# One load over 128 partitions, an earlier first product, and paired half-width products in a three-stage kernel

## The chip, the cores and the metric

The kernel runs on one core of a Trainium2 chip. The metric is the device time in microseconds of one execution. The time before is the median of three runs. A profile of one execution, taken by the hardware profiler, goes with it.

The engines are called TensorE (PE in the profile; PEld is its weight load), VectorE (DVE), ScalarE (ACT), GpSimd (POOL) and SyncE (SP). SyncE issues most of the transfers here.

## The reference

The reference has three stages. The first is a gated linear attention with a state per batch and head; the second sends each token to one of eight experts; the third is a dense gated block.

```python
B, H, S, D = 4, 8, 768, 48
f = 1.0 / (1.0 + np.exp(-f_logit))
for t in range(S):
    state = f[:, :, t, :, None] * state + np.einsum('bhd,bhe->bhde', k[:, :, t], v[:, :, t])
    y[:, :, t] = np.einsum('bhd,bhde->bhe', q[:, :, t], state)
x = y.transpose(0, 2, 1, 3).reshape(3072, 384)
...
logits = normalized(x) @ normalized(expert_emb).T / tau          # 8 experts
expert_idx = argmax(logits); gate_w = softmax(logits)[expert_idx]
out[tokens of e] = gate_w * (relu(x @ w1[e]) @ w2[e])            # 384 -> 1024 -> 384
...
return (out @ w_a) * (out @ w_b) @ w_out                         # 384 -> 1536 -> 384
```

All inputs and the output are float32.

## The kernel before

**Stage 1, attention (until about 137 us).** The 768 positions of 4 batches are cut into 24 blocks of 128 positions, numbered g = 0 to 23: chunk g // 4 of batch g % 4. A block holds 8 heads in 4 pairs; the two heads of a pair lie in partitions 0 to 47 and 64 to 111. The order of the work on each engine is written out by hand, and each engine works through its own list in that order.

For block g: `load_a` (L188) brings q, k and f, two transfers of 48 partitions each, into a ring of four tiles whose remaining partitions are filled once by memsets (`clear`, L552). `load_b` (L196) brings v. `tanh` (L202) and `gate_f` (L206) make the gate from f; the second of them runs on ScalarE for the first three blocks and on GpSimd after. `scan_b` (L218) is a backward scan on VectorE and, on GpSimd, the scaled k (kt). `scan_r` (L229) is a forward scan, `q_scale` (L237) the scaled q (qc), both on VectorE. `scores` (L269) makes two banks of scores on TensorE, one per head of a pair. `mask_a` (L279) copies one bank on ScalarE and masks it on GpSimd; `mask_v` (L292) masks the other on VectorE. `turn_k` (L253) transposes kt, `evac_k` (L262) copies the transpose out. `inter` (L300) is the product with the state, `intra` (L307) that of the masked scores with v, both into one bank, which `evac_y` (L314) copies out. `u_part` (L319) makes the addition to the state; `s_scale` (L244) and `s_add` (L328) update the state. `turn_y` (L337) turns the block's output so that tokens lie in partitions, and makes the eight logits with it. `x_copy` (L367) copies the rows out, `x_sq` (L361) makes each row's sum of squares on ScalarE, `x_lg` (L372) the logits.

The loop starts at L629. Iteration g does the scans of block g + 2, the scores and masks of g + 1, the products of g and the turn of g - 1. A few blocks at a time form a round: `route` (L385), a list of small VectorE steps with a few rank products on TensorE, which `tick` (L542) advances a step at a time, finds each token's place; `scatter_row` (L456) then sends 128 rows to `slots` in memory by an indirect transfer on GpSimd's queue. Before that, `zero_fill` (L623) has written zeros to parts of `slots`. Between them, weights of the first expert are loaded (`w_load`, L116) and split in two parts (`w_hi` on ScalarE, `w_lo` on VectorE).

The kernel starts with memsets, first loads, and 18 products on constants (`warm_up`, L347). Then come the scans of blocks 0 and 1 and the scores of block 0, before the loop is entered.

**Early experts (about 137 to 158 us).** The first 224 rows of expert 0 are worked on while the last rows are still on their way: `early_h` (L499), `early_split` (L507), `early_y` (L512), in turn for j = 0 to 7, between them the last round, the counts of all experts (L747 to L749) and the order of the experts.

**Stage 2, experts (L1103, 64 steps), and stage 3 (L1229).** A step of stage 2 has a product with w1 (`h_part`), its relu on ScalarE and a remainder on VectorE (`h_split`, L1006), and the product of the step before with w2 (`y_part`, L1020). Rows of the next expert are loaded from `slots` and turned meanwhile (`rows_load`, `x_turn`, `ids_copy`).

Of the kernel before, what the change touches and what calls it, by code (L numbers as in the profile page):

```python
# [18 lines left out]
L = 128  # L19
# [29 lines left out]
def build(tc, I, out, dbg=None):  # L49
# [23 lines left out]
    ids0 = epool.tile([HP, 2, XO], F32, name="ids0")  # L73
    half = epool.tile([128, NT // 128], F32, name="half")
    a0 = epool.tile([128, KC, XT], F32R, name="a0")
    XE = [a0[:, :, i * EN:(i + 1) * EN] for i in range(2)]
    pcs = epool.tile([1, 2, 128], F32, name="pcs")
# [65 lines left out]
    with tc.manual_schedule():  # L143
# [44 lines left out]
        def load_a(g, eng=(SP, SP), parts=False):  # L188
            if g < NG:
                qkf = qkf_t[g % NQ]  # L190
                for c in ((slice(2, 3), slice(0, 2)) if parts else (slice(0, 3),)):
                    for i in range(2):
                        eng[i].dma_start(out=qkf[64 * i:64 * i + D, c], in_=I["qkf"][g, i, :, c])
                st[g] = dict(qkf=qkf)

        def load_b(g, eng=SP):  # L196
            if g < NG:
                vx = in_p.tile([128, H, D], F32, tag="vx", name="vx", bufs=4)
                eng.dma_start(out=vx, in_=I["vx"][g])
                st[g].update(vx=vx)  # L200

        def tanh(g):  # L202
            if g < NG:
                A.activation(out=Fb[g % 2][:, :, 0:L], in_=st[g]["qkf"][:, 2], func=ACTF.Tanh, scale=0.5)

        def gate_f(g):  # L206
            if g < NG:
                F = Fb[g % 2]
                if g < 3:
# [8 lines left out]
        def scan_b(g):  # L218
            if g >= NG:
# [3 lines left out]
            V.tensor_tensor_scan(out=fl(Bt)[:, ::-1], data0=Fx[g % 2][:, 1:n1 + 1][:, ::-1], data1=fl(pat)[:, ::-1],  # L223
                                 initial=0.0, op0=ALU.mult, op1=ALU.add)
# [67 lines left out]
        def mask_v(g):  # L292
# [3 lines left out]
            pm = at_p.tile([128, NP, L], F32, tag="pm0", name="pm0")  # L296
            V.tensor_tensor(out=pm, in0=d["ps"][0], in1=mask.unsqueeze(1).to_broadcast([128, NP, L]), op=ALU.mult)
            d["pm0"] = pm
# [38 lines left out]
        def turn_y(g):  # L337
# [6 lines left out]
            for p in range(NP):  # L344
                T.matmul(out=xt[:, p], lhsT=d["yS"][:, p], rhs=pick[0:HP, p], start=True, stop=True)
# [21 lines left out]
        def x_copy(g, rd):  # L367
            i, xt = rd["n"], st[g]["x"]
# [69 lines left out]

        def rows_load(e):
# [48 lines left out]
        def early_turn():  # L488
            V.tensor_copy(ids0, rows[0:HP, 0:2, 0:XO])
# [51 lines left out]

        def tick(n=1):  # L542
# [9 lines left out]
        def clear(i, *eng):  # L552
            for c, e in zip((2, 1, 0), eng):
                e.memset(qkf_t[i][:, c], 30.0 if c == 2 else 0.0)

        V.memset(qkf_t[0][:, 2], 30.0)
        G.memset(qkf_t[0][:, 0:2], 0.0)
        load_a(0, (SP, A), True)
# [17 lines left out]
        clear(2, G, G, G)  # L576
        load_a(2)
        load_b(1)
# [6 lines left out]
        clear(3, G, G, G)  # L585
# [7 lines left out]
        q_scale(0)  # L593
        tanh(1)
# [847 lines left out]
```

## Time and profile before

| | |
|---|---|
| median of 3 runs | 831.11 us (829.69 to 831.29) |
| the profiled execution | 832.62 us, its span 830.9 us |
| mean granted TensorE clock | 0.994 of full |
| TensorE busy | 810.6 us (98%) |
| VectorE, ScalarE, GpSimd busy | 397.7, 331.1, 222.3 us |
| moved by DMA | 76.74 MB, mean 92 GB/s |

A row of the timeline gives the start, the duration, the engine, the line, the tiles (out<-in) and shapes, and in square brackets how long the engine was idle before it and what ended that. Instructions of one kind that follow each other are merged (x16). A row of windows gives the busy time of each engine in a stretch, in the order PE, PEld, DVE, ACT, POOL, then the granted clock as a share of full speed, the mean busy share of the 16 DMA engines, and GB/s.

### The profile page before, as it was taken

How to read it: one execution, taken by the hardware profiler on the slowest of the kernel's cores; microseconds unless marked ns; L12 is line 12 of the kernel's file. 1: busy time of each engine (PE TensorE's matmuls, PEld its weight loads, DVE VectorE, ACT ScalarE, POOL GpSimd, SP SyncE). 2: the span in 40 equal slices, each digit the busy share in tenths (PEclk: the TensorE clock that was granted, in tenths of full speed). 3: DMA queues.
4: the chain of work that ended last, by engine and by line, in shares of the span. 5: the costliest groups of instructions: out<-in, count | busy, mean ns of one | idle time of the engine just before them, and what ended most of it. 6: DMA issues, size and time to landing. Idle time of an engine off the chain costs nothing. (4 is left out here: it accounts for less than half of the span.)

```text
span 830.9 us, 13077 instructions
## 1 busy us (share of the span) xinstructions
PE 810.6 (98%) x5156; PEld 727.7 (88%) x5156; DVE 397.7 (48%) x696; ACT 331.1 (40%) x636; POOL 222.3 (27%) x237
## 2 busy tenths in 40 slices
PE   6999999999999999999999999999999999999996
PEld 4888888999999999998888888888888888888886
DVE  7999996545555454487873213212322321222222
ACT  4787885354544554444442122222221222222211
POOL 6648674235454644440001000100010010001001
PEclk8999999999999999999999999999999999999999
DMA  9999962554465545433411000100010010001001
GB/s 177 233 283 244 217 188 78 181 163 146 153 180 189 163 134 179 156 91 109 136 53 39 0 1 1 39 0 1 1 39 1 0 39 1 1 0 39 1 1 41
DMA packets 38490, 76.74 MB, mean 92 GB/s; under 512 B 7481, under 2 KB 20391, under 8 KB 38423
## 3 DMA queue, kind: packets, MB, share of 16 engines
q1 hardware_dynamic: 35223, 65.99, 28.5%
q0 software_dynamic: 3072, 9.56, 3.3%
q8 instruction: 42, 0.69, 0.3%
q10 hardware_dynamic: 128, 0.30, 0.1%
q14 instruction: 25, 0.20, 0.1%
HBM read 63.58 MB, written 12.25 MB: 91 GB/s over the span
## 5 line engine op out<-in xcount | busy, mean ns | idle before, releaser
L988 PE MATMUL pa<-a,w 128*128 128x512 f32 (+1 forms) x438 | 171.8, 392 | 0.0
L987 PE MATMUL pa<-a,w 128*128 128x512 f32 (+1 forms) x438 | 171.6, 392 | 0.0
L989 PE MATMUL pa<-a,w 128*128 128x512 f32 (+1 forms) x438 | 171.5, 392 | 0.0
L1175 DVE TENSOR_TENSOR rows<-rows,pa 128x512 f32<-128x512 f32 (+1 forms) x73 | 49.6, 679 | 241.3 <-PE pa L989 234.9
L1205 POOL DMA_INDIRECT out<-yT,idx x24 | 23.5, 979 | 430.4 <-ACT yT L1203 424.0
L1169 ACT ACTIVATE rows<-pa 128x512 f32<-128x512 f32 (+1 forms) x73 | 43.3, 593 | 168.8 <-PE pa L989 168.7
L1176 ACT ACTIVATE gh<-rows 128x512 fp32r<-128x512 f32 x71 | 44.9, 633 | 149.4 <-DVE rows L1175 149.4
L989 PEld LDWEIGHTS pa<-a,w 128*128 128x128 f32 x438 | 82.3, 188 | 19.3
L987 PEld LDWEIGHTS pa<-a,w 128*128 128x128 f32 x438 | 82.3, 188 | 16.1
L988 PEld LDWEIGHTS pa<-a,w 128*128 128x128 f32 x438 | 82.1, 187 | 16.2
L1192 PE MATMUL pq<-w,gl 128*128 128x384 f32 x284 | 95.3, 336 | 0.0
L1191 PE MATMUL pq<-w,gh 128*128 128x384 f32 x284 | 95.3, 336 | 0.0
L1190 PE MATMUL pq<-w,gh 128*128 128x384 f32 x284 | 95.3, 336 | 0.0
L867 POOL TENSOR_TENSOR w<-raw,w 128x512 fp32r<-128x512 f32 x48 | 73.0, 1543 | 40.6 <-ACT w L864 36.0
L1030 PE MATMUL po<-hh,w 128*128 128x224 f32 (+7 forms) x384 | 80.3, 344 | 0.0
L1179 DVE TENSOR_TENSOR gl<-rows,gh 128x512 fp32r<-128x512 f32 x71 | 49.1, 691 | 44.1 <-ACT gh L1176 42.7
L1030 PEld LDWEIGHTS po<-hh,w 128*128 128x128 f32 x384 | 66.6, 189 | 1.5 <-ACT hh L1010 0.3
L987 PE MATMUL ph<-a,w 128*128 128x224 f32 (+7 forms) x192 | 65.5, 341 | 0.1
L989 PE MATMUL ph<-a,w 128*128 128x224 f32 (+7 forms) x192 | 65.3, 340 | 0.0
L988 PE MATMUL ph<-a,w 128*128 128x224 f32 (+7 forms) x192 | 65.3, 340 | 0.0
L1010 ACT ACTIVATE hh<-ph 128x224 fp32r<-128x224 f32 (+7 forms) x64 | 31.5, 492 | 81.2 <-PE ph L989 78.2
L1011 DVE SCALAR_TENSOR_TENSOR hl<-ph,hh 128x224 fp32r<-128x224 f32 (+7 forms) x64 | 35.7, 558 | 45.4 <-ACT hh L1010 44.8
(245 smaller groups left out, 1326.8 us busy)
## 6 DMA issues: line engine op xcount, KB each, us to landing
raw<-moe_w SPq DMA_DIRECT2D x32, 768.0 KB
qkf<-qkf SPq DMA_DIRECT2D x44, 288.0 KB
vx<-vx SPq DMA_DIRECT2D x24, 192.0 KB
raw<-moe_w_a SPq DMA_DIRECT2D x6, 768.0 KB
raw<-moe_w_b SPq DMA_DIRECT2D x6, 768.0 KB
raw<-moe_w_out SPq DMA_DIRECT2D x6, 768.0 KB
slots<-raw SPq DMA_DIRECT2D x8, 295.5 KB
rows<-slots SPq DMA_DIRECT2D x2, 344.8 KB
```

Of the source, the lines that this page charges most:

```text
L867: (G if i < NPOOL else V).tensor_tensor(out=wt[:, 1, f], in0=raw[:, f], in1=wt[:, 0, f].bitcast(F32), op=ALU.subtract)
L987: T.matmul(out=out, lhsT=wh, rhs=xh, start=first, stop=False)
L988: T.matmul(out=out, lhsT=wl, rhs=xh, start=False, stop=False)
L989: T.matmul(out=out, lhsT=wh, rhs=xl, start=False, stop=last)
L1030: T.matmul(out=OS[e][k], lhsT=w[:, j % 4, k * 128:(k + 1) * 128], rhs=x, start=(j == 0 and w is wh and x is hh), stop=(j == FJ - 1 and x i ...
L1169: A.activation(out=ab[:, r], in_=pa, func=ACTF.Copy)
L1175: V.tensor_tensor(out=ab[:, r], in0=ab[:, r], in1=pp[1], op=ALU.mult)
L1176: A.activation(out=gh[:, r], in_=ab[:, r], func=ACTF.Copy)
L1179: V.tensor_tensor(out=gl[:, r], in0=ab[:, r], in1=gh[:, r].bitcast(F32), op=ALU.subtract)
L1190: T.matmul(out=q, lhsT=gh[:, c], rhs=wh[:, f % 4], start=(f == 0), stop=False)
L1191: T.matmul(out=q, lhsT=gh[:, c], rhs=wl[:, f % 4], start=False, stop=False)
L1192: T.matmul(out=q, lhsT=gl[:, c], rhs=wh[:, f % 4], start=False, stop=(f == F2J - 1))
```

## The change

- q, k and f of a block come in one transfer over 128 partitions; the host's layout holds the remaining partitions, so that the memsets go. Block 0's f comes in two halves, and `tanh`, `gate_f` and the first `scan_b` work on halves.
- The first `intra`, `evac_y` and `u_part` stand before the loop. `turn_k` and `evac_k` move one iteration earlier, next to `scores`; `mask_a(0)` and `evac_k(0)` go ahead of `tanh(2)`.
- `inter` and `turn_y` are split in two products per pair of heads, each with half of the columns of the weights.
- For 12 blocks (`alt`) the second mask goes from VectorE to ScalarE and GpSimd, and the gate from GpSimd to ScalarE. Splits of weights move between iterations, two of them to GpSimd.
- The sums of squares are taken later, on the rows as they come back from memory (`row_sq`).
- Rows are scattered one per iteration, until iteration 20.
- In the early experts, splits 0 and 1 run on VectorE, and some steps change places.

```diff
-        def load_a(g, eng=(SP, SP), parts=False):
+        def load_a(g, *cs):
             if g < NG:
                 qkf = qkf_t[g % NQ]
-                for c in ((slice(2, 3), slice(0, 2)) if parts else (slice(0, 3),)):
-                    for i in range(2):
-                        eng[i].dma_start(out=qkf[64 * i:64 * i + D, c], in_=I["qkf"][g, i, :, c])
-                st[g] = dict(qkf=qkf)
+                for c in cs or ((slice(0, 3),),):
+                    SP.dma_start(out=qkf[(slice(None),) + c], in_=I["qkf"][(g, slice(None)) + c])
+                st.setdefault(g, {}).update(qkf=qkf)
...
-        def gate_f(g):
+        def gate_f(g, r=slice(0, NP)):
             if g < NG:
-                F = Fb[g % 2]
-                if g < 3:
+                F = Fb[g % 2][:, r]
+                if g < 3 or alt(g - 3):
                     A.activation(out=F[:, :, 0:L], in_=F[:, :, 0:L], func=ACTF.Copy, scale=0.5, bias=0.5)
...
-            V.tensor_tensor_scan(out=fl(Bt)[:, ::-1], data0=Fx[g % 2][:, 1:n1 + 1][:, ::-1], data1=fl(pat)[:, ::-1],
-                                 initial=0.0, op0=ALU.mult, op1=ALU.add)
+            for lo, hi in ((n1 // 2, n1), (0, n1 // 2)) if g == 0 else ((0, n1),):
+                V.tensor_tensor_scan(out=fl(Bt)[:, lo:hi][:, ::-1], data0=Fx[g % 2][:, 1 + lo:1 + hi][:, ::-1],
+                                     data1=fl(pat)[:, lo:hi][:, ::-1], initial=0.0, op0=ALU.mult, op1=ALU.add)
...
@@ mask_v @@
+            if alt(g - 1):
+                A.activation(out=pm, in_=d["ps"][0], func=ACTF.Copy)
+                G.affine_select(out=pm, in_=pm, pattern=[[0, NP], [1, L]], base=0, channel_multiplier=-1,
+                                compare_op=ALU.is_ge, fill=0.0)
+                return
...
@@ inter @@
-                    T.matmul(out=y_full[0:HP, p], lhsT=S_t[g % B][:, p], rhs=d["qc"][:HP, p],
-                             start=(p == 0), stop=False, skip_group_check=True)
+                    for i in range(2):
+                        r = slice(64 * i, 64 * i + D)
+                        T.matmul(out=y_full[r, p], lhsT=S_t[g % B][:, p, r], rhs=d["qc"][:HP, p],
+                                 start=(p == 0), stop=False, skip_group_check=True)
...
@@ turn_y @@
-                T.matmul(out=xt[:, p], lhsT=d["yS"][:, p], rhs=pick[0:HP, p], start=True, stop=True)
+                for i in range(2):
+                    r = slice(64 * i, 64 * i + 64)
+                    T.matmul(out=xt[r, p], lhsT=d["yS"][:, p, r], rhs=pick[0:HP, p], start=True, stop=True)
...
-        def x_sq(g, rd):
+        def x_copy(g, rd):
             i, xt = rd["n"], st[g]["x"]
             st[g]["at"] = (rd, i)
-            junk = x_p.tile([128, NP, 2 * D], BF16, tag="junk", name="junk", bufs=1)
-            A.activation(out=junk, in_=xt[:, :, 0:2 * D], func=ACTF.Square, accum_out=rd["xb"][:, i, 1:2])
...
+        def row_sq(e, P, *js):
+            for j in js:
+                row = rows_of(e)[0:P, j]
+                A.activation(out=sq_junk[0:P], in_=row[:, XO:RW], func=ACTF.Square, accum_out=row[:, 1:2])
...
@@ early_split @@
-            A.activation(out=hh, in_=EP[j], func=ACTF.Relu)
+            if j < 2:
+                V.tensor_scalar(out=hh, in0=EP[j], scalar1=0.0, scalar2=None, op0=ALU.max)
+            else:
+                A.activation(out=hh, in_=EP[j], func=ACTF.Relu)
...
+        def alt(g):
+            return 6 <= g <= 19 and g not in (9, 12)
...
@@ ahead of the loop @@
-        V.memset(qkf_t[0][:, 2], 30.0)
-        G.memset(qkf_t[0][:, 0:2], 0.0)
-        load_a(0, (SP, A), True)
+        f_, qk, up, down = (slice(2, 3),), (slice(0, 2),), slice(2, NP), slice(0, 2)
+        load_a(0, f_ + (up,), f_ + (down,), qk)
...
-        clear(1, V, V, V)
-        load_a(1, (SP, SP), True)
+        load_a(1, f_, qk)
         SP.dma_start(out=emb, in_=I["embp"])
...
+        load_a(2, f_)
         load_b(0)
+        load_a(2, qk)
+        load_b(1)
+        load_a(3, f_, qk)
+        load_b(2)
...
-        tanh(0)
-        gate_f(0)
-        load_a(3)
-        load_b(2)
+        for r in (up, down):
+            tanh(0, r)
+            gate_f(0, r)
         scan_b(0)
         scan_r(0)
         q_scale(0)
...
-        tanh(2)
-        gate_f(2)
...
         scores(0)
...
+        turn_k(0)
+        mask_a(0)
+        scan_b(1)
+        evac_k(0)
+        tanh(2)
+        gate_f(2)
         A.activation(out=en, in_=en_ps, func=ACTF.Copy)
-        turn_k(0)
-        scan_b(1)
...
-        mask_a(0)
         mask_v(0)
         scan_r(1)
         q_scale(1)
+        intra(0)
+        evac_y(0)
+        u_part(0)
...
@@ the loop @@
             scan_b(g + 2)
+            tanh(g + 3)
+            if alt(g):
+                gate_f(g + 3)
             scores(g + 1)
+            turn_k(g + 1)
             if fresh and g < NG - 1:
                 tick()
-            evac_k(g)
-            tanh(g + 3)
-            if g == NG - 2:
-                w_lo(V, 3)
             mask_a(g + 1)
...
             mask_v(g + 1)
             if fresh and g < NG - 1:
                 tick(2)
-            gate_f(g + 3)
+            if not alt(g):
+                gate_f(g + 3)
+            evac_k(g + 1)
             s_scale(g + 2)
...
             inter(g)
             if g == NG - 1:
                 tick()
-            intra(g)
-            evac_y(g)
+            if g > 0:
+                intra(g)
+                evac_y(g)
...
-            for _ in range(2 if len(scaled) > 3 or g >= 20 else 1):
+            for _ in range(2 if g >= 20 else 1):
                 scatter_row()
...
                 x_copy(g - 1, rd)
-                x_sq(g - 1, rd)
...
-            if g in (4, 5, 6, 12, 13, 14, 18, 19, 20):
+            if g in (4, 5, 9, 12, 13, 16, 18, 20, 21):
                 w_hi(1)
-            if g in (5, 6, 7, 13, 14, 15):
+            if g in (5, 6):
+                w_lo(G, 1)
+            if g in (10, 13, 16, 17):
                 w_lo(V, 1)
...
-            turn_k(g + 1)
-            u_part(g)
+            if g > 0:
+                u_part(g)
             if g == NG - 2:
                 x_lg(g - 1)
+                w_lo(V, 3)
...
@@ the end of the stage @@
         early_h(0)
+        early_split(0)
         bg.append(route(dict(rd, n=3, last=True)))
         tick(6)
-        early_split(0)
         x_copy(NG - 1, rd)
-        x_sq(NG - 1, rd)
         early_h(1)
-        it[0] = NG
-        tick(1)
         early_split(1)
         early_y(0)
-        tick(2)
+        it[0] = NG
+        tick(3)
...
         V.tensor_reduce(out=amp, in_=al_all, axis=AX.XY, op=ALU.min)
+        early_h(2)
         pc = fl(ps_x.tile([128, NP, XW], F32, tag="x", name="pc"))
...
         T.transpose(pc[1][0:1], amp, ident)
-        early_h(2)
...
         early_split(3)
+        row_sq(0, HP, 0)
...
         early_split(4)
+        row_sq(0, HP, 1)
...
         early_out()
+        row_sq(0, HP, 2, 3)
...
@@ a step of stage 2 @@
+            n = 4 if e == 0 else 3
+            if 0 <= j - 3 < n and e + 1 < NE:
+                row_sq(e + 1, CAPS[e + 1] // 4, *[i for i in range(4) if min(i, n - 1) == j - 3])
-            if j == 5:
+            if j == n + 2:
                 ids_copy(e + 1)
...
@@ the host's layout @@
-    qkf = np.empty((NCH, B, 2, D, 3, NP, L), q.dtype)
+    qkf = np.zeros((NCH, B, 2, 64, 3, NP, L), q.dtype)
     for j, a in enumerate((q, k, f)):
-        qkf[:, :, :, :, j] = a.reshape(B, NP, 2, NCH, L, D).transpose(3, 0, 2, 5, 1, 4)
+        qkf[:, :, :, 0:D, j] = a.reshape(B, NP, 2, NCH, L, D).transpose(3, 0, 2, 5, 1, 4)
+    qkf[:, :, :, D:64, 2] = qkf[:, :, :, 0:64 - D, 2]
```

## Rows read from the trace of the kernel before

**Rows 1.** Windows, by stage: window, length, busy us (x) per engine, clock, DMA, GB/s.

```profile
21.11:34.75 13.64, 12.35 (x180) 10.72 (x181) 13.12 (x23) 11.49 (x31) 8.83 (x37) 1.00 1.04 213
34.75:129.33 94.58, 91.56 (x1205) 79.91 (x1205) 89.23 (x169) 77.28 (x205) 63.14 (x73) 1.00 0.87 229
...
158.00:830.90 672.90, 665.62 (x3415) 602.47 (x3415) 263.86 (x417) 221.74 (x352) 129.10 (x93) 1.00 0.21 68
```

**Rows 2.** Timeline 0 to 22: start, us, engine, line, tiles, shapes, [idle before].

```profile
1.50 2.84 SPq L193 DMA_DIRECT2D qkf<-qkf  x6
...
4.27 0.63 ACT L204 ACTIVATE F<-qkf 128x512 f32<-128x512 f32 x1 [0.33 <-DMA qkf<-qkf]
...
5.59 1.23 DVE L223 TENSOR_TENSOR_SCAN Bt<-F,resets 128x516 f32<-128x516 f32 x1 [0.54 <-ACT F L210]
...
9.23 1.16 PE L277 MATMUL pp<-qc,kt 64*128 64x128 f32 x16 [1.53 <-DVE qc L242]
...
13.70 0.63 ACT L204 ACTIVATE F<-qkf 128x512 f32<-128x512 f32 x1 [3.31 <-DMA qkf<-qkf]
...
15.59 2.07 PE L277 MATMUL pp<-qc,kt 64*128 64x128 f32 x14 [1.67 <-ACT pm L287]
...
21.11 1.16 PE L277 MATMUL pp<-qc,kt 64*128 64x128 f32 x16 [0.52 <-DVE qc L242]
```

**Rows 3.** DMA view, 10 to 20 us.

```profile
DMA packets 600, 1.84 MB, mean 184 GB/s; under 512 B 109, under 2 KB 365, under 8 KB 600
```

**Rows 4.** DMA view, 200 to 205 us, in 40 slices.

```profile
GB/s 360 442 360 459 395 585 269 353 303 252 151 202 303 101 151 151 303 50 151 252 202 101 403 151 101 151 353 101 151 0 51 0 0 0 0 0 0 0 25 61
```

**Rows 5.** Windows, the stretch at half clock.

```profile
12.25:19.08 6.83, 4.25 (x29) 3.64 (x31) 3.90 (x8) 3.36 (x7) 3.73 (x4) 0.50 1.08 191
```

**Rows 6.** Timeline of PEld, one block of the loop.

```profile
78.86 0.97 PEld L277 LDWEIGHTS pp<-qc,kt 64*128 64x128 f32 x16
79.95 0.93 PEld L304 LDWEIGHTS y_ps<-qc,S 112*112 112x112 f32 x8
81.01 0.83 PEld L311 LDWEIGHTS y_ps<-pm,vx 128*48 128x48 f32 x16
82.02 0.97 PEld L345 LDWEIGHTS x_ps<-pick,yS 112*128 112x128 f32 x8 [0.18 <-issue]
82.89 0.44 PEld L259 LDWEIGHTS kv<-ident,kt 112*128 112x128 f32 x4
83.47 0.44 PEld L325 LDWEIGHTS u_ps<-vx,ktT 128*48 128x48 f32 x16
```

**Rows 7.** Windows, that block.

```profile
78.86:83.97 5.11, 5.11 (x73) 4.48 (x69) 5.02 (x8) 4.22 (x13) 4.21 (x5) 1.00 1.04 307
```

**Rows 8.** Timeline of that block, ScalarE and VectorE.

```profile
78.48 0.48 ACT L365 ACTIVATE junk<-x_ps 128x384 bf16<-128x384 f32 x1
...
78.85 0.20 ACT L365 ACTIVATION_READ_ACCUMULATOR junk<-x_ps 128x1 f32 x1
...
80.77 0.68 DVE L297 TENSOR_TENSOR pm<-pp,mask 128x512 f32<-128x512 f32 x1
```

**Rows 9.** Timeline 50 to 70, first scatter and stall.

```profile
58.70 1.24 POOL L459 DMA_INDIRECT slots<-xb,posi  x1 [4.18 <-DVE S L335]
...
62.50 1.16 PE L277 MATMUL pp<-qc,kt 64*128 64x128 f32 x16 [1.53 <-POOL kt L226]
```

**Rows 10.** Timeline of PE, end of the attention stage.

```profile
138.28 1.27 PE L505 MATMUL u_ps<-a,w 128*128 128x224 f32 x9
...
141.73 0.48 PE L521 MATMUL kv<-he,w 128*128 128x224 f32 x2 [0.76 <-ACT he L509]
...
143.84 0.17 PE L747 MATMUL pc<-run,ones 128*1 128x8 bf16 x1 [0.85 <-DVE run L437]
```

**Rows 11.** Timeline of the expert stage.

```profile
229.30 0.52 ACT L1010 ACTIVATE hh<-ph 128x432 fp32r<-128x432 f32 x1
...
231.74 1.34 PE L1030 MATMUL po<-hh,w 128*128 128x432 f32 x6
```

More of the change, by code (lines that the diff above doesn't have):

```diff
@@ L73, in build @@
     ids0 = epool.tile([HP, 2, XO], F32, name="ids0")
+    sq_junk = epool.tile([HP, DM], BF16, name="sq_junk")
     half = epool.tile([128, NT // 128], F32, name="half")
@@ L76, in build @@
     XE = [a0[:, :, i * EN:(i + 1) * EN] for i in range(2)]
-    pcs = epool.tile([1, 2, 128], F32, name="pcs")
+    pcs = epool.tile([1, 2 * NE + 128], F32, name="pcs")
     off_f = epool.tile([1, 2, NE], F32, name="off_f")
@@ L199, in load_b, with tanh @@
                 eng.dma_start(out=vx, in_=I["vx"][g])
-                st[g].update(vx=vx)
-        def tanh(g):
+                st.setdefault(g, {}).update(vx=vx)
+        def tanh(g, r=slice(0, NP)):
             if g < NG:
-                A.activation(out=Fb[g % 2][:, :, 0:L], in_=st[g]["qkf"][:, 2], func=ACTF.Tanh, scale=0.5)
-        def gate_f(g):
+                A.activation(out=Fb[g % 2][:, r, 0:L], in_=st[g]["qkf"][:, 2, r], func=ACTF.Tanh, scale=0.5)
+        def gate_f(g, r=slice(0, NP)):
             if g < NG:
-                F = Fb[g % 2]
-                if g < 3:
+                F = Fb[g % 2][:, r]
+                if g < 3 or alt(g - 3):
                     A.activation(out=F[:, :, 0:L], in_=F[:, :, 0:L], func=ACTF.Copy, scale=0.5, bias=0.5)
@@ L488, in early_turn @@
         def early_turn():
-            V.tensor_copy(ids0, rows[0:HP, 0:2, 0:XO])
             kv = ps_k.tile([128, 512], F32, tag="kv", name="kv")
@@ L575, in build @@
         V.memset(half, 0.5)
-        clear(2, G, G, G)
-        load_a(2)
-        load_b(1)
         G.memset(ident, 1.0)
@@ L593, in build @@
         q_scale(0)
+        A.activation(out=y_full, in_=warm.rearrange("p (a b) -> p a b", a=NP), func=ACTF.Copy)
+        A.activation(out=u_full, in_=warm[:, 0:NP * HP].rearrange("p (a b) -> p a b", a=NP), func=ACTF.Copy)
         tanh(1)
@@ L639, in build @@
                 zero_fill(2 * g - 5)
-            if g in (2, 10, 11, 17):
+            if g in (2, 10, 11, 18):
                 w_load()
             if g == 22:
+                assert not scaled
                 early_load()
             scan_b(g + 2)
+            tanh(g + 3)
+            if alt(g):
+                gate_f(g + 3)
             scores(g + 1)
+            turn_k(g + 1)
             if fresh and g < NG - 1:
                 tick()
-            evac_k(g)
-            tanh(g + 3)
-            if g == NG - 2:
-                w_lo(V, 3)
             mask_a(g + 1)
@@ L664, in build @@
                 V.reciprocal(out=en, in_=en)
-                V.tensor_tensor(out=pick[:, :, 2 * D:XW], in0=emb, in1=en.unsqueeze(1).to_broadcast([128, NP, NE]),
+                G.tensor_tensor(out=pick[:, :, 2 * D:XW], in0=emb, in1=en.unsqueeze(1).to_broadcast([128, NP, NE]),
                                 op=ALU.mult)
@@ L704, in build @@
                         G.memset(lims[:, i, e:e + 1], float(v))
+                G.memset(xb_all[:, :, 1], 0.0)
                 G.iota(out=xb_all[:, :, 0].rearrange("p (c b) -> p c b", b=B), pattern=[[L, NCH], [S, B]], base=0,
@@ L749, in build @@
         T.transpose(pc[1][0:1], amp, ident)
-        early_h(2)
-        V.tensor_copy(pcs[:, 0, 0:2 * NE], pc[0][0:1, 0:2 * NE])
+        V.tensor_copy(pcs[:, 0:2 * NE], pc[0][0:1, 0:2 * NE])
         w_hi(1)
@@ L755, in build @@
         big = [1, 7, 7]
-        V.scalar_tensor_tensor(out=key[:, 0], in0=pcs[:, 0, 1:NE], scalar=float(NE), in1=prio[0:1, 1:NE],
+        V.scalar_tensor_tensor(out=key[:, 0], in0=pcs[:, 1:NE], scalar=float(NE), in1=prio[0:1, 1:NE],
                                op0=ALU.mult, op1=ALU.add)
@@ L772, in build @@
         early_split(3)
-        V.tensor_tensor(out=won, in0=place_f, in1=pcs[:, 0, 1:NE].unsqueeze(1).to_broadcast(big), op=ALU.mult)
+        row_sq(0, HP, 0)
+        V.tensor_tensor(out=won, in0=place_f, in1=pcs[:, 1:NE].unsqueeze(1).to_broadcast(big), op=ALU.mult)
         V.tensor_reduce(out=srt[:, 0, 1:NE], in_=won, axis=AX.X, op=ALU.add)
-        V.tensor_copy(srt[:, 0, 0:1], pcs[:, 0, 0:1])
+        V.tensor_copy(srt[:, 0, 0:1], pcs[:, 0:1])
         early_y(2)
@@ L786, in build @@
         early_split(5)
+        V.tensor_copy(ids0, rows[0:HP, 0:2, 0:XO])
         early_y(4)
@@ L789, in build @@
         early_split(6)
-        V.tensor_copy(pcs[:, 1], pc[1][0:1])
+        V.tensor_copy(pcs[:, 2 * NE:], pc[1][0:1])
         early_y(5)
@@ L1120, in build @@
                     rows_load_n(e + 2)
-            if j == 6 and e + 1 < NE:
+            if j == n + 3 and e + 1 < NE:
                 ids_store(e + 1)
@@ L1415, in layout @@
         "gv": gv.reshape(S // GT, 2, GT * B * NP * D),
-        "qkf": qkf.reshape(NCH * B, 2, D, 3, NP, L),
+        "qkf": qkf.reshape(NCH * B, 128, 3, NP, L),
         "vx": vx.reshape(NCH * B, L, H, D),
```

15 lines of the change are left out of this document (3 added, 12 removed).

## The prediction

> **What bounds the kernel now.** I read the stage windows first, then the timeline of the start, the DMA view, one block of the loop by instruction, and the end of the attention stage. From 158 us on, TensorE is busy 665.62 of 672.90 us [rows 1] and the change removes no product there, so the whole question lies in the first 158 us. The reader is to see four stretches.
>
> The start, until scores(2) at 21.11 [rows 2], is bound by transfers and by queue order: tanh(2) waits 3.31 us for its f, and the copy that frees the score banks stands behind it on ScalarE, so most of scores(1) starts only at 15.59.
>
> From 21.11 to 34.75 VectorE is busy 13.12 of 13.64 us [rows 1]: three blocks of 4.5 us, bound by VectorE.
>
> From 34.75 to 129.33 (18 blocks) TensorE bounds. One block takes 5.11 us, without a gap, while VectorE is busy 5.02 and ScalarE 4.22 [rows 7]. The starts of its six groups [rows 6] give scores 1.09, inter 1.06, intra 1.01, turn_y 0.87, turn_k 0.58, u_part 0.50. Eighteen such blocks, less turn_k in the last three and u_part in the last two, are 18 x 5.11 - 3 x 0.58 - 2 x 0.50 = 89.2 us; the stretch takes 94.58. The other 5.4 are the rank products of four rounds, which stay, and waits. The largest: the first scatter sits 4.18 us on GpSimd behind the zero fills' landing, kt queues behind it, and TensorE idles 1.53 us [rows 9].
>
> The end: early_y(0) waits 0.76 us for ScalarE, the counts 0.85 us for VectorE, and early_h(2) stands behind both [rows 10].
>
> **The change part by part.**
>
> *Loads.* A q, k, f load over 2 x 48 partitions ran at 184 GB/s with the DMA engines full [rows 3]; a weight load, which fills 128 partitions, has slices of 360 to 460 GB/s [rows 4]. A block grows from 0.59 to 0.79 MB: 3.2 us before, 0.79/0.36 = 2.2 us after if it gets the second rate, 4.3 us if it keeps the first. I take 360, because the rows differ in their partitions and not in their direction. The memsets of the padding go; the first load waited for one until 1.50 [rows 2].
>
> *Start.* With that wait gone, and half of f per load, I put the first tanh at 3.0 instead of 4.27 (bounds 2.6 and 4.27). In halves, the scan starts after two half passes on ScalarE instead of two whole ones. Together scores(0) comes at 7.8 instead of 9.23. From there VectorE paces: scan_b(1), mask_v(0), scan_r(1), qc(1), scan_b(2), mask_v(1), the reciprocal, scan_r(2) and qc(2) are four scans of 1.23 [rows 2], four products of 0.68 [rows 8] and small ones, about 8.4 us, plus 0.5 where scan_b(2) waits for F(2), whose tanh(2) now stands behind mask_a(0) and evac_k(0) on ScalarE. So scores(2) falls at 16.6. By 360 GB/s all loads up to block 2's f (1.8 MB) are in by 8 us, so no transfer is late there; at 184 they are in at 12.5, which costs 2 us. [...] I allow 0.4 us: scores(2) at 17.0, **-4.1 us** (bounds -5.2 and -1.5). The three blocks behind it stay VectorE's: 0.
>
> *TensorE per block.* inter and turn_y go from eight full-width passes to sixteen half-width ones that run in pairs, as intra already does, and turn_k moves between scores and inter. turn_y's eight loads with no change of shape behind them take 0.87, or 0.109 each. inter, with eight of the same, takes 1.06, and intra, sixteen in pairs, 1.01: 0.19 and 0.14 are lost where the shape of the tile changes, and turn_y's first weight load idles 0.18 there [rows 6]. After the change inter, intra, turn_y and u_part have one shape; the gap before u_part moves to before inter. That saves 0.19 + 0.14 = 0.33, and up to 0.16 more as turn_y streams 104 columns, not 128 (0.87 x 24/128). From the other side, if pairing buys nothing, inter costs intra's 1.01 and so does turn_y: +0.09. I take -0.38, as intra is the nearest row: 18 x 0.38 = **-6.8 us** (bounds -8.8 and +1.6).
>
> [...]
>
> *Who follows.* In the 18 blocks VectorE is busy 89.23 us [rows 1]; 12 masks and 2 weight splits leave it, 14 x 0.68: 79.7. ScalarE is busy 77.28; it loses 18 squares of 0.68 (0.48, and 0.20 for reading the sum [rows 8]) and gains 12 mask copies and 12 gates of about 0.62: 79.9. TensorE's sum is 89.2 - 6.8 = 82.4 plus the rank products. So TensorE still bounds, but two engines stand within 3%. GpSimd gains 12 affine selects and loses 12 gates. The first scatter should no longer wait: the zero fills queue behind faster loads. I give back 2 us for that stall, and charge 1 us for waits among three nearly full engines: **-1.0 us** (bounds -3 and +4).
>
> *End.* early_split(0) goes ahead of route and to VectorE, early_h(2) ahead of the counts. Before, early_h(2) began behind the counts of 143.84, 5.7 us after early_h(0) at 138.28 [rows 10]. After: early_h(0), early_h(1) and early_y(0) back to back (3 x 1.1), the rank products 0.6, early_h(2), then the counts: early_y(1) comes 1.3 us earlier: **-1.3 us** (bounds -2 and 0).
>
> *Squares.* 32 squares of 0.68 move to ScalarE in the early and expert stages. The relu of 229.30 ended 1.9 us ahead of its reader at 231.74 [rows 11], and ScalarE is busy 221.74 of 672.90 [rows 1]: that idle time hides them. In the first expert, whose steps are short, I charge +0.1 us (bounds 0 and +1.5).
>
> **Sum.** -4.1 - 6.8 - 1.0 - 1.3 + 0.1 = -13.1 us on the profiled execution's 832.62: 819.5. That execution was 1.5 us over the median of the runs shown (831.11), so 818.0.
>
> **The rivals.**
> 1. *The block does not shorten*: each half-width pass carries a fixed cost that eats the saving, or ScalarE or VectorE holds the block near 5.1. For it: both are within 3% of TensorE. Against: intra's pairs. Without the 6.8: -13.1 + 6.8 = -6.3, 825. [...]
> 2. *Everything lands at its good bound* in start and blocks: -5.2 - 8.8 - 1.0 - 1.3 = -16.3, 815 or a little less.
> 3. *The clock*: the lower level lies over scores(2) to scores(4), where blocks have 0.5 us to spare. scores at half clock took 2.07 for 14 passes against 1.16 for 16 [rows 2], so two blocks of 4 us become 8: +3, 821.
> 4. *Slower: the squares in the expert stage*. Each stands on ScalarE ahead of the next relu. It decides from the point where a relu ends less than 0.68 us before its reader needs it; then each of the 28 squares of experts 1 to 7 delays TensorE by 0.68, +19 us, and the sum is +6: 837. Against: the 1.9 us.
> 5. *The loads keep 184 GB/s*, so that the change does not do what it says: block inputs of 0.98 MB take 5.3 us, above 5.11: the block gives back what the start gains (1.5), about 831.
>
> **How the numbers follow.** Forecast (815 to 823) 0.55; rival 1 0.19; rival 2 0.08; rival 3 0.08; rival 4 0.05; rival 5 0.05. The predicted time is 818. The range runs from 811, below rival 2 by its error, to 826, just over rival 1. About 0.2% (1.7 us) is what a measurement can tell from no change. Faster: all but rivals 4 and 5 with a little of rival 1, 0.90; same 0.04; slower 0.06.
>
> **What would show each step.** Scores(2) before 18 us and no wait of tanh(2) on a transfer: the start. Block starts 4.7 to 4.8 us apart in the loop, no idle before turn_y's weight load: the pairs. Blocks of 5.0 with TensorE idle: ScalarE or VectorE took over. The first scatter without a wait of 4 us: the zero fills. early_h(2) less than 5 us after early_h(0): the end. TensorE idle in the expert stage behind a relu, or DMA rates near 184 GB/s while q, k, f load, would make the prediction wrong.

## The result and the profile after

The changed kernel takes 821.24 us in the median of 4 runs (819.47 to 821.87), the kernel before 831.2 beside it: a ratio of 0.9865, 95% interval 0.9836 to 0.9895. A second group, on another chip, gave 818.52 against 829.71, or 0.9867 (0.9845 to 0.9889). The forecast was 818.0 after 831.11, or 0.984: faster by 13.1 us where 10.0 and 11.2 were measured. The first profiled execution took 821.87 us, its span 819.9.

The windows of the kernel after, in the columns of [rows 1]:

```profile
17.04:30.84 13.80, 12.84 (x205) 11.55 (x205) 13.23 (x23) 10.23 (x25) 9.01 (x39) 0.88 0.81 270
30.84:117.46 86.62, 82.42 (x1493) 76.42 (x1494) 84.50 (x154) 79.71 (x194) 65.14 (x74) 1.00 0.81 274
148.15:819.90 671.75, 664.29 (x3415) 601.42 (x3415) 262.20 (x417) 236.90 (x412) 128.73 (x93) 1.00 0.22 68
```

The first row runs from scores(2) to scores(5), the second to scores(23). The 18 blocks take 86.62 us instead of 94.58; TensorE's work in them fell by 9.1 us, its idle time rose from 3.0 to 4.2. The expert stage is 1.15 us shorter, though the same products run in it. Between the last two rows 30.69 us pass; from scores(23) at 129.33 to 158.00 [rows 1] it was 28.67.

The start, in the timeline of the kernel after, beside [rows 2] and [rows 5]:

```profile
3.06 0.42 ACT L204 ACTIVATE F<-qkf 128x256 f32<-128x256 f32 x1 [0.75 <-DMA qkf<-qkf]
...
7.97 1.16 PE L278 MATMUL pp<-qc,kt 64*128 64x128 f32 x16 [1.09 <-DVE qc L243]
...
11.03 0.62 ACT L204 ACTIVATE F<-qkf 128x512 f32<-128x512 f32 x1
...
17.04 1.27 PE L278 MATMUL pp<-qc,kt 64*128 64x128 f32 x16 [2.42 <-DVE qc L243]
18.25 1.01 PE L260 MATMUL kv<-ident,kt 112*128 112x112 f32 x4
19.18 1.95 PE L319 MATMUL y_ps<-pm,vx 128*48 128x128 f32 x16
```

The first tanh is at 3.06 (forecast 3.0), scores(0) at 7.97 (7.8); tanh(2) at 11.03 waits for no transfer; scores(2) is at 17.04 (17.0). Intra(1) ran at a granted clock of 0.50 (window 19.18 to 21.13): 1.95 us for what takes 1.05 later. The DMA view from 10 to 20 us, beside [rows 3]:

```profile
DMA packets 1200, 3.81 MB, mean 381 GB/s; under 512 B 132, under 2 KB 527, under 8 KB 1199
```

One plain block, weight loads and then its window, beside [rows 6, 7]:

```profile
79.71 0.97 PEld L278 LDWEIGHTS pp<-qc,kt 64*128 64x128 f32 x16
80.81 0.39 PEld L260 LDWEIGHTS kv<-ident,kt 112*128 112x128 f32 x4
81.34 0.82 PEld L312 LDWEIGHTS y_ps<-qc,S 112*48 112x48 f32 x16
82.14 0.90 PEld L319 LDWEIGHTS y_ps<-pm,vx 128*48 128x48 f32 x16
83.02 0.79 PEld L355 LDWEIGHTS x_ps<-pick,yS 112*64 112x64 f32 x16
83.75 0.49 PEld L333 LDWEIGHTS u_ps<-vx,ktT 128*48 128x48 f32 x16
```

```profile
79.71:84.30 4.59, 4.59 (x88) 4.27 (x84) 4.49 (x9) 4.56 (x11) 3.65 (x4) 1.00 0.80 272
```

From start to start: inter 0.80 (before 1.06), intra 0.88 (1.01), turn_y 0.73 (0.87), turn_k 0.53 (0.58), u_part 0.55 (0.50). The gap of 0.18 ahead of turn_y is gone. The block lost 0.52 us; TensorE, ScalarE and VectorE are all full.

GpSimd's first scatter, beside [rows 9]; no stall of TensorE follows it:

```profile
51.33 1.24 POOL L469 DMA_INDIRECT slots<-xb,posi  x1 [1.28 <-DMA qkf<-qkf]
```

The end of the attention stage on TensorE, beside [rows 10], and the window from early_y(1) to early_y(2):

```profile
125.72 0.41 PE L491 MATMUL kv<-ident,rows 112*128 112x112 f32 x2 [1.22 <-DMA rows<-slots]
...
127.31 1.26 PE L514 MATMUL u_ps<-a,w 128*128 128x224 f32 x9
...
131.07 1.24 PE L514 MATMUL u_ps<-a,w 128*128 128x224 f32 x9
133.38 0.17 PE L765 MATMUL pc<-run,ones 128*1 128x8 bf16 x1 [1.06 <-DVE run L442]
...
135.21 2.12 PE L514 MATMUL y_ps<-a,w 128*128 128x224 f32 x9
```

```profile
133.57:137.13 3.56, 3.56 (x21) 3.56 (x20) 2.52 (x12) 0.00 (x0) 2.71 (x3) 0.56 0.19 71
```

The turn of the early rows now waits 1.22 us for their transfer, which it did not before; the counts wait 1.06; then the clock falls to 0.56 of full, so that early_y(1) and early_h(3) take 3.56 us instead of 2.01. Here the first execution lost what the forecast put down as a gain.

A relu of the expert stage and its reader, beside [rows 11]:

```profile
220.08 0.52 ACT L447 ACTIVATE sq_junk<-rows 104x384 bf16<-104x384 f32 x1
...
220.60 0.51 ACT L1031 ACTIVATE hh<-ph 128x432 fp32r<-128x432 f32 x1
...
221.94 0.74 PE L1051 MATMUL po<-hh,w 128*128 128x432 f32 x3
```

The squares push the relu back: it ends 0.83 us ahead of its reader (1.9 before). Over the 64 relus of this stage most end 2 to 3.6 us ahead; the least is 0.25 us, twice, in one case where it was 1.40 before. The view of waits shows no wait of TensorE behind a relu in this profile.

### The profile page after: what moved, and what is told of

The parts are those of the page before. It is cut to its first block, busy times and chain, and to the rows that moved or that the text cites. A ratio compares the mean times of both kernels' runs of the same rounds, so it can differ in the third digit from the quotient of the medians.

```text
span 819.9 us, 13733 instructions
## 1 busy us (share of the span) xinstructions
PE 799.0 (97%) x5508; PEld 722.9 (88%) x5508; DVE 389.9 (48%) x680; ACT 347.1 (42%) x676; POOL 221.8 (27%) x234
## 5 line engine op out<-in xcount | busy, mean ns | idle before, releaser
L1215 PEld LDWEIGHTS pq<-w,gh 128*128 128x128 f32 x284 | 53.3, 188 | 3.3
```

The lines of the kernel that those rows point to most:

```text
L1215: T.matmul(out=q, lhsT=gh[:, c], rhs=wl[:, f % 4], start=False, stop=False)
```

## The experiments

e1 to e4, e5 to e8 and e9 to e12 each shared a chip and its runs of the kernel before. A window or a timeline comes from one execution of each kernel.

**e1, the pairs alone on the kernel before** (turn_y likewise):

```diff
-                    T.matmul(out=y_full[0:HP, p], lhsT=S_t[g % B][:, p], rhs=d["qc"][:HP, p],
+                    for i in range(2):
+                        r = slice(64 * i, 64 * i + D)
+                        T.matmul(out=y_full[r, p], lhsT=S_t[g % B][:, p, r], rhs=d["qc"][:HP, p],
```

> The kernel before with one edit: inter and turn_y as sixteen half-width passes. Theory: TensorE's work of a plain block falls by 0.3 to 0.5 us (5.11 to 4.6-4.8), but VectorE was busy 5.02 of the 5.11 there, so it holds the blocks at about 5.0 and most of the gain is not paid out: TensorE idles behind qc, blocks of 4.95 to 5.05, time 1 to 3 us below the kernel before. Rival A: the pairs pay out by themselves, blocks of 4.7, time 7 us lower. Rival B: a half-width pass carries a fixed cost and the group of inter takes 1.06 or more: time within 1 us of before.

Measured: 830.56 against 832.61, ratio 0.9981 (0.9961 to 1.0001). The loop's window:

```profile
34.21:126.65 92.44, 85.11 (x1493) 76.77 (x1494) 89.84 (x168) 76.78 (x206) 63.77 (x73) 1.00 0.87 233
```

Plain blocks take 4.72, not the 4.95 to 5.05 that I expected of VectorE; TensorE's work fell by 6.45 us. But the loop gained only 2.1: 7.3 us are idle now, 3.0 before. The pairs do what they should, and are not paid.

**e2, the loads alone on the kernel before** (with the layout of the inputs; the memsets go):

```diff
-                    for i in range(2):
-                        eng[i].dma_start(out=qkf[64 * i:64 * i + D, c], in_=I["qkf"][g, i, :, c])
+                    eng[0].dma_start(out=qkf[:, c], in_=I["qkf"][g, :, c])
```

> The kernel before with one edit: q, k and f of a block loaded by one transfer over 128 partitions, with its padding from memory, and the memsets of the padding left out. Theory: the transfers run at 300 GB/s or more in the first 20 us (184 before), the first tanh comes at 3 us, tanh(2) waits less, and the 4.18 us wait of the first scatter and the 1.53 us stall of TensorE behind it go, since the zero fills land earlier: scores(2) 1.5 to 2.5 us earlier, 3 to 4 us in all. Rival: the rate belongs to the direction and stays near 184 GB/s, so the larger blocks come later: 0 to +15 us.

Measured: 828.69, ratio 0.9956 (0.9939 to 0.9973), as the theory has it, though the first tanh came at 3.72 and not at 3. Scores(2) came at 19.04, scores(23) at 124.59 (129.33 before). The DMA view from 10 to 20 us, and the first scatter:

```profile
DMA packets 918, 3.20 MB, mean 320 GB/s; under 512 B 111, under 2 KB 494, under 8 KB 917
```

```profile
52.74 1.30 POOL L458 DMA_INDIRECT slots<-xb,posi  x1 [0.94 <-DVE Rt L233]
```

The window moved 320 GB/s with one transfer over 128 partitions for each two over 48, and 184 before, in the same direction: the rate goes with the form of the transfer. Partitions and number of transfers were not tried apart. The scatter's 4.18 us wait [rows 9], 0.94 here, goes with the slow loads. That it came from the zero fills behind them fits their issue: the last two go out from 49.38 us in the kernel before, from 41.47 in the changed one, whose first scatter waits 1.28.

**e9, both on the kernel before:**

> The kernel before with both single edits: half-width pairs (alone 0.9981) and one load over 128 partitions (alone 0.9956). Theory: pairs alone paid 2 us of the 7 that the plain blocks (4.72 instead of 5.11) promise, because TensorE waited 5.8 us in the loop for qc, most of it behind the first scatters that wait for the zero fills; faster loads take those waits away, so the two together give more than their sum of 5.7: 7 to 10 us below the kernel before, ratio 0.988 to 0.9915. Rival: the waits come from VectorE and ScalarE, which mask, gate and square as before; the two give their sum or less, ratio 0.993 or more.

Measured: 825.88 against 830.42, ratio 0.9933 (0.9909 to 0.9957), no more than the sum. The rival holds: with the scatters early, TensorE still idles 5.4 us in the loop, 3.9 of it behind VectorE's qc.

```profile
32.16:122.39 90.23, 84.83 (x1494) 76.60 (x1494) 87.63 (x168) 77.46 (x207) 64.04 (x73) 1.00 0.78 266
```

**e5, the changed kernel again** (no edit):

> The changed kernel itself, as the control for the kernels of this group and for e3 and e4. If the stretch at half clock behind the counts belongs to the kernel, it is there again (3 to 4 us at about half clock between early_h(0) and early_h(5), early_h(3) taking about 2 us); if it is an accident of one execution, the end takes 1.5 us less than in the first profile. The wait of 1.2 us for the rows should be there in any case, since the order of the scatters makes it.

Measured: 818.52, ratio 0.9867. The whole end at full clock, and its lines on TensorE:

```profile
117.48:144.55 27.07, 26.24 (x298) 24.77 (x298) 15.93 (x60) 10.02 (x27) 9.11 (x9) 1.00 0.37 124
```

```profile
125.23 0.41 PE L491 MATMUL kv<-ident,rows 112*128 112x112 f32 x2 [0.72 <-DMA rows<-slots]
...
126.82 1.26 PE L514 MATMUL u_ps<-a,w 128*128 128x224 f32 x9
...
130.27 1.24 PE L514 MATMUL u_ps<-a,w 128*128 128x224 f32 x9
131.44 0.17 PE L765 MATMUL pc<-run,ones 128*1 128x8 bf16 x1
```

The counts wait for nothing and the end takes 27.07 us, 1.60 less than before. Most of what the first profile's 30.69 has more belonged to that execution; the wait for the rows is the kernel's, since both have it.

**e3, the changed kernel with full-width inter and turn_y** (e1's edit undone):

> The changed kernel with inter and turn_y back at eight full-width passes. Theory: the pairs are what shortened the block, since TensorE bounds it after the other edits too: plain blocks of 5.0 to 5.1 us instead of 4.59, 18 of them and the end +7 to +9 us, near 829. Rival: the block is short because masks left VectorE, and blocks stay under 4.75: less than +3 us.

Measured: 824.40 against 832.61, ratio 0.9910 (0.9883 to 0.9936). The theory's blocks (5.08), but not its time:

```profile
30.70:121.72 91.02, 90.99 (x1206) 79.94 (x1206) 84.81 (x154) 80.60 (x194) 65.78 (x74) 1.00 0.76 260
121.72:149.52 27.80, 26.70 (x259) 25.32 (x259) 16.02 (x60) 10.13 (x27) 8.67 (x9) 1.00 0.36 121
```

TensorE has no idle time in the loop at all. Undoing the pairs costs 8.6 us of work there and 4.4 to 4.9 of time, since the changed kernel idles 3.8 to 4.2. By the ratios it is 0.0043, some 3.6 us; these are of two groups, whose intervals overlap.

**e7, without the alternation of mask and gate:**

```diff
-            return 6 <= g <= 19 and g not in (9, 12)
+            return False
```

> The changed kernel with the mask of pm0 on VectorE and the gate on GpSimd in every block, as before. Theory: VectorE, which was busy 5.02 us a block before, holds the 12 blocks at about 4.85 to 5.0 us instead of 4.59 while TensorE idles behind qc: +3 to +5 us against the changed kernel. Rival: VectorE has enough left at 4.6 us a block: within 0.5 us.

Measured: 823.32, 4.8 us over e5 in the same group (ratio 0.9914). The time is the theory's:

```profile
32.08:122.65 90.57, 82.65 (x1493) 76.53 (x1494) 88.46 (x166) 71.60 (x171) 61.26 (x75) 1.00 0.77 258
```

TensorE idles 7.9 us in the loop, and nearly all of it ends with a step of VectorE. But the loss is not spread over the 12 blocks at 4.85 to 5.0 us each: several keep their 4.58, and the blocks with steps of route take up to 6.12 (5.57 in the first profile).

**e8, the squares back in the attention stage:**

```diff
+            A.activation(out=junk, in_=xt[:, :, 0:2 * D], func=ACTF.Square, accum_out=rd["xb"][:, i, 1:2])
...
-            for j in js:
+            for j in ():
```

> The changed kernel with the squares of the rows back beside x_copy, in the attention stage on ScalarE, and none in the early and expert stages. Theory: ScalarE gains 0.68 us a block in which it is busy some 4.1 to 4.4 of 4.59 us, becomes the bound in the blocks with mask copy and gate, and these take 4.8 to 5.1: +3 to +6 us against the changed kernel, while the expert stage gains nothing (671 to 673 us as it is). Rival A: the squares fit, within 0.5 us. Rival B: the squares in the expert stage cost TensorE time there, which comes back: 1 us or more faster.

Measured: 821.59, 3.1 us over e5 (ratio 0.9899). The loop and the expert stage:

```profile
31.32:120.39 89.07, 82.55 (x1494) 76.43 (x1494) 85.31 (x154) 86.71 (x231) 67.50 (x74) 1.00 0.78 265
149.87:821.20 671.33, 664.29 (x3415) 601.38 (x3415) 262.28 (x417) 222.38 (x352) 128.97 (x93) 1.00 0.22 68
```

ScalarE is busy 86.71 of 89.07, and the loop takes 2.9 us more than e5's 86.12. The expert stage without the squares took 671.33, with them 671.55 (e5) and 671.75, and TensorE has no wait behind a relu in either of these two that the view of waits shows. A cost of a few tenths is not excluded: e10's profile has one such wait, of 0.3 us.

**e6, matmuls that compute nothing in three idle places:**

```diff
+                fill(fl(ps_x.tile([128, NP, XW], F32, tag="x", name="fx")), 9)   # behind turn_k(1)
...
+        fill(resets[:, 0:512], 5)                                               # ahead of early_turn
...
+        fill(resets[:, 0:512], 4)                                               # behind early_h(2)
```

> The changed kernel with matmuls that compute nothing put into three idle places of TensorE: 9 behind turn_k(1) where scores(2) waits 2.4 us for VectorE, 5 ahead of the turn that waits 1.2 us for the rows, 4 ahead of the counts that wait 1.1 us. Theory: the idle places are what lets the clock fall to half; filled, scores(2) to scores(3) takes 4.5 to 4.9 us instead of 5.27 and the 1.5 us lost behind the counts come back: 1.5 to 2.5 us below the changed kernel. Rival: the clock falls for another reason, and the fillers are work put into waits: within 0.5 us, or slower by up to 1 us where a filler outlasts its wait.

Measured: 819.46, 0.9 us over e5 (ratio 0.9877): the rival's time, for a reason of its own. The clock did stay at 1.00 from 5.6 to 814.6 us, and the mean granted clock is 0.997 or 0.998 in all six runs; of the 49 runs of the changed kernel and its other edits 5 reach that. So the fillers hold the clock. The starts of scores(2) to scores(4):

```profile
16.98 1.16 PE L278 MATMUL pp<-qc,kt 64*128 64x128 f32 x16 [0.84 <-DVE qc L243]
...
21.90 1.16 PE L278 MATMUL pp<-qc,kt 64*128 64x128 f32 x16 [1.15 <-DVE half L725]
...
26.34 1.16 PE L278 MATMUL pp<-qc,kt 64*128 64x128 f32 x16 [0.66 <-DVE qc L243]
```

Scores(2) to scores(3) takes 4.92 us instead of 5.28, near what the theory had, but the next block 4.44 instead of 4.10: VectorE paces, TensorE at full clock waits for it, and scores(5) stands at 30.77 as at 30.84. This stretch alone does not show the fillers at work: e10 has none there and the clock was full too, while in e4, e7 and e11 it was low for twice as long as in the first profile. Scores(2) to scores(3) in e10, then in e4:

```profile
16.79:21.71 4.92, 3.78 (x68) 3.41 (x69) 4.49 (x9) 3.36 (x7) 3.29 (x6) 1.00 0.77 286
18.90:25.60 6.70, 6.70 (x69) 6.12 (x69) 5.56 (x10) 2.23 (x5) 3.54 (x5) 0.52 0.61 194
```

Scores(2) to scores(5) took 13.78 us in e10, 13.80 in e5 and the first profile, but 14.99 to 15.15 in e4, e7 and e11. At the end it took 18.67 us from early_h(0) to the expert stage against e5's 17.73, within what the same order takes without fillers (17.73 to 19.12, see e10), so that the price of the fillers is not told apart there.

**e10, the end's order as before** (both first splits have their first half on ScalarE again):

```diff
         early_h(0)
-        early_split(0)
         bg.append(route(dict(rd, n=3, last=True)))
         tick(6)
+        early_split(0)
...
-        early_h(2)
         pc = fl(ps_x.tile([128, NP, XW], F32, tag="x", name="pc"))
...
+        early_h(2)
```

> The changed kernel with the end's order as before: early_split(0) behind the first steps of route, both first splits with their first half on ScalarE, early_h(2) behind the counts; the squares stay in the early stage. Theory: that order is worth 1.3 to 1.6 us (the control took 27.07 us from scores(23) to the first expert, the kernel before 28.66): 28.3 to 28.8 here, +1.3 to +1.6 us in all. Rival: the gain of the end came from the narrower turn_y and the squares that left, and the order is worth under 0.5 us.

Measured: 822.39, ratio 0.9893 (0.9866 to 0.9920).

```profile
116.97:147.50 30.53, 26.50 (x299) 24.84 (x299) 15.51 (x58) 10.75 (x29) 9.03 (x9) 1.00 0.32 110
```

The end takes 30.53 us at full clock, 3.5 more than e5's. Of this, 1.0 comes ahead of early_h(0), where the rows landed later (1.75 us of wait) and this edit has no part. From early_h(0) to the experts it took 20.15 us, and 19.72 in the kernel before (158.00 - 138.28); with the new order, in the five profiles at full clock without an edit there (e3, e5, e7, e11, e12), 17.73 to 19.12. The kernel before with single edits (e1, e2, e9) keeps the old order and took 19.12 to 19.70. So the old order took 19.12 to 20.15, 19.56 in the mean of five profiles, and the new one 18.48: some 1.1 us, near the 1.3 forecast. But the ranges touch, and the rival's 0.5 us is not excluded.

**e4 and e12, earlier scatters:**

```diff
-            for _ in range(2 if g >= 20 else 1):
+            for _ in range(2 if len(scaled) > 3 or g >= 20 else 1):
```

This is e4; e12 has `2 if g >= 19 else 1` there.

> The changed kernel with one line back: two rows are scattered per block as soon as more than three wait, instead of only from block 20 on. In the changed kernel the last scatter before the rows of expert 0 are read falls after scores(22), the read is issued at 121.25 and TensorE waits 1.22 us for it before the turn at 125.72; 1.06 us of idle follow before the counts, and then 3.6 us at a clock of 0.56. Theory: the late scatters are why the end gave nothing: with this line the read is issued 3 us earlier, the 1.22 us wait goes, and the stretch at half clock, which cost 1.5 us, goes with it: 1.2 to 2.8 us below the changed kernel, about 819. Rival A: only the wait goes, the clock still falls: -1.2. Rival B: the earlier scatters delay kt on GpSimd inside the loop and TensorE pays there what the end gains: within 0.5 us.

> The changed kernel with two rows scattered per block from block 19 on instead of 20, so that the last scatter ahead of the rows' read is one earlier. Theory: the read is issued some 1.3 us earlier and the wait of 0.7 to 1.2 us at the turn shrinks to under 0.2; unlike e4 no block of the loop with mask and gate on GpSimd beyond one gets a second scatter, so the loop stays within 0.3 us: 0.5 to 0.9 us below the changed kernel, which only the trace can show. Rival: the extra scatter delays one kt by as much, 0.

Measured: e4 824.59, ratio 0.9903 (0.9877 to 0.9930); e12 818.83, 0.9852 (0.9820 to 0.9885). Loop and end of each, e4's first:

```profile
33.91:121.78 87.87, 82.45 (x1493) 76.46 (x1494) 85.81 (x154) 79.97 (x195) 67.87 (x75) 1.00 0.82 270
121.78:130.34 8.56, 8.52 (x141) 7.53 (x141) 5.98 (x19) 3.71 (x9) 1.81 (x3) 1.00 0.18 52
130.34:153.38 23.04, 20.83 (x160) 20.10 (x158) 10.76 (x43) 6.29 (x19) 5.81 (x6) 0.85 0.33 109
```

```profile
31.29:117.88 86.59, 82.29 (x1494) 76.37 (x1494) 84.54 (x154) 79.77 (x195) 66.48 (x75) 1.00 0.83 277
117.88:145.55 27.67, 26.68 (x298) 24.83 (x298) 16.47 (x61) 9.99 (x27) 8.62 (x9) 1.00 0.33 114
```

In both the wait for the rows goes: from scores(23) to early_h(0) 8.56 in e4 and 8.55 in e12, against 9.34 in e5. That is the theory's part. But e4's loop is 1.25 to 1.75 us longer than the changed kernel's two, e12's 0.47 longer than e5's, and neither end as a whole is shorter than e5's; in e4 the clock fell there for 6.8 us, in the first profile for 3.4. Neither beats the changed kernel by a measurable amount. Since e4's clock fell without the wait, the wait is not needed for that.

**e11, loads of blocks 4 to 23 over 2 x 48 partitions:**

```diff
-                    SP.dma_start(out=qkf[(slice(None),) + c], in_=I["qkf"][(g, slice(None)) + c])
+                    for r in (slice(None),) if cs else (slice(0, D), slice(64, 64 + D)):
+                        SP.dma_start(out=qkf[(r,) + c], in_=I["qkf"][(g, r) + c])
```

> The changed kernel with the loads of blocks 4 to 23 as two transfers over 48 partitions each, without the padding (which the first four loads leave in the buffers); the start keeps its transfers. Theory: a transfer over 48 partitions runs near 184 GB/s, so a block's 0.59 MB take 3.2 us of DMA time, and with rows, zero fills and weights the DMA engines are full for the 4.6 us of a block: the first scatter waits again behind the zero fills, 1.5 to 4 us slower, most of it before 70 us. Rival: 3.2 us fit in 4.6, and only the start needed the rate: within 0.5 us.

Measured: 820.82, ratio 0.9874 (0.9847 to 0.9901), not told apart from the changed kernel.

```profile
17.29:32.44 15.15, 14.30 (x204) 13.00 (x205) 13.32 (x23) 9.96 (x25) 9.08 (x39) 0.78 1.03 219
32.44:119.08 86.64, 82.42 (x1493) 76.43 (x1494) 84.52 (x154) 79.72 (x194) 65.13 (x75) 1.00 0.91 240
```

The loop is as the first profile's 86.62, and the first scatter waits 1.33 us, as there. As far as the interval goes the rival holds: the rate pays in the start. Scores(2) to scores(5) took 1.35 more, with the clock low for 6.8 us instead of 3.4. That belongs to the execution: e4 and e7, whose loads are the changed kernel's, have it too.

## Why the prediction was right

The direction and the two large terms, start and blocks, held; the smaller ones of waits and end did not come out as worked out, and the time missed by 3.2 us of 821. By its own steps, on the profiled executions (before 832.62):

```
term                          forecast  first profile  control e5
start, to scores(2)             -4.1       -4.07         -3.55
scores(2) to scores(5)           0         +0.16         +0.16
the 18 blocks                   -7.8       -7.96         -8.46
end, scores(23) to experts      -1.3       +2.02         -1.60
expert stage                    +0.1       -1.15         -1.35
sum                            -13.1      -11.00        -14.80
```

The last column overstates the change. The control's profile is its fastest run, 818.01, on a chip where the kernel before took 829.71 in the median, and it is set against the 832.62 of the first chip; by the medians the two kernels differ by 10.0 and 11.2.

*Start.* Right in its size and its parts. The loads alone give 2.07 of it (e2); the other 2.0, put down to the new order, were not tried by themselves. No run shows the 0.4 us that I allowed for the clock: in the first profile it was 1.00 from 0 to 17.04, and in e6, which held it beyond that, scores(2) came at 16.98 all the same. In e4 it fell earlier, to 0.80 in the mean from 9.20 to 18.90, and scores(0) to scores(2) took 9.67 us for 9.07; how much of that is the clock's was not tried. The stretch from scores(0) that VectorE paces took 9.07 us instead of 8.9.

*TensorE per block.* Mis-sized. I took -0.38, from intra as the nearest row; the block lost 0.52, just past the good bound of 0.49. Of that bound, 0.16 had no ground: turn_y streams 104 columns in the kernel before as well (112x104 in its trace). The same edits alone gave 0.39 (e1); the rest came with turn_k's move, which without the pairs gave no more than 0.03 (e3, 5.08 for 5.11): turn_y took 0.92 in e1, with turn_k behind it, and 0.73 here, with u_part of its own shape behind it. That time is lost at a change of shape was my estimate from [rows 6]: these times fit it, and what costs the time there was not shown. A fixed cost of a half-width pass that eats the saving (rival 1) does not show: inter took 0.80 us with sixteen loads and 1.06 with eight.

*Who follows.* Wrong in sign. The stall of 1.5 us went as forecast (e2), but TensorE's idle time in the loop rose by 1.2 us instead of falling by 1.0, since the block had come down to 4.59 where VectorE needs 4.49 and ScalarE 4.56. ScalarE came out as added up (79.71 us for 79.9), but VectorE was busy 84.50 us of the 18 blocks where the sum had 79.7. The step that failed is to take off a mask's whole 0.68 us and leave VectorE's other steps at their price: q_scale took 0.69 to 0.75 us in 11 of the 18 blocks and 0.98 to 1.65 in the other 7, and in just these a select or a weight split had begun on GpSimd within 0.4 us before it. In the kernel before it was 3 of 18, behind the gate. So part of what left VectorE for GpSimd came back there; that GpSimd is the cause was not tried. One such block of the first profile, and a free one:

```profile
82.84 0.63 POOL L289 TENSOR_SCALAR_AFFINE_SELECT pm<-pm 128x512 f32<-128x512 f32 x1 [0.59 <-ACT pm L288]
82.97 1.05 DVE L243 TENSOR_TENSOR qc<-qkf,Rt 128x512 f32<-128x512 f32 x1
...
112.65 0.75 DVE L243 TENSOR_TENSOR qc<-qkf,Rt 128x512 f32<-128x512 f32 x1
```

The idle time took back what the pairs gave too much, so -7.8 came out by luck, by two errors of opposite sign. What the followers are worth shows in e7 (4.8 us), e8 (3.1) and e9: without them, pairs and loads give 4.5 us of the 10 to 11.

*End.* The order gave about what was forecast (-1.60 for the whole end in the control; some 1.1 in the means of e10), but I overlooked one edit: the diff also drops the second scatter per iteration before block 20. That makes the rows late by 0.72 to 1.22 us, seen in e4 and e12, which bring it back. The +2.02 of the first profile holds, besides that wait, 1.55 us at the lower clock, which e5 does not have.

*Squares.* Right as far as e8 resolves it. The fourth rival's condition came near in single steps, where a relu ended 0.25 us ahead of its reader and, in e10, TensorE waited 0.3 us; but most steps have 2 us or more left, so that its 0.68 for each of 28 squares could not add up.

*Expert stage.* The 1.15 and 1.35 us were not forecast. The stage took 672.6 to 673.3 us in the four profiles of the kernel before and its edits, and 671.3 to 672.4 in nine of the ten of the changed kernel and its edits (673.1 in e10), with the same products in it. So scatter of executions alone does not fit well; what in the changed program shortens it stays open. It is not the squares: e8, without them there, has the 671.3.

The rivals: the block did shorten (1); the good bounds together (2) were not reached, since the start stopped at -4.07 of -5.2 and the idle time took back what TensorE's work gave; the clock (3), half of full in [rows 5], fell in the stretch it described, in some executions for 6.8 us, where it cost 1.2 to 1.35 us by scores(5), in others for 3.4 us or not at all, where VectorE paced and it cost nothing, and it cost 1.55 us at the end, where I had not looked; (4) and (5) fell with e8 and e2.

## What to carry to other kernels

A shorter block on the bounding engine is paid only as far as the next engines are relieved with it: here the pairs alone took 6.45 us of work away and gave 2. An engine that hands work over may keep part of it, as VectorE did with a q_scale of 0.98 to 1.65 us in 7 of 18 blocks, 0.69 to 0.75 in the others: read its busy time again after the move. Work moved past the end of a stage has to be followed to its last transfer: one scatter fewer per iteration made the rows 0.72 to 1.22 us late at the turn. And one profile is one execution: repeat it before a microsecond in it is explained.

## What the runs showed that was not expected

The clock falls in the end stage in some executions of the same program: to 0.56 over 3.56 us in the first profile, not at all in e5 (1.00 over the whole end). Among the edited kernels it fell longer in e4 (6.8 us), once more in e8 (from 130.2 for 3.4 us), and not in e3, e7, e10, e11 and e12. In the start it is the same: low for 3.4 us in the first profile, e5, e8 and e12, for 6.8 in e4, e7 and e11 (in e4 once more before that, 0.80 in the mean from 9.20 to 18.90), not at all in e3 and e10, with the same instructions on TensorE in all of these but e3. Filled idle places kept it up in all six runs of e6; what decides it without them stays open.

In the same place instructions that read TensorE's products start late, by amounts that vary. Counted from the start of early_h(0), the split that waits for it alone starts after 1.30 us in e3, e5 and e7, 1.62 in the first profile, 2.39 in e12, and 3.04 in the kernel before, where early_h(0) had ended after 1.27 (there the profile puts the wait down to rank products that ended at 2.69). So part of the waits in [rows 10], which I took for an effect of the order, is of this kind. In each of these profiles, also those with 1.30, four scatters in a row are issued on GpSimd meanwhile; so these alone do not decide it, and whether they have a part was not tried.
